# A memory-augmented attention and a squared-ReLU layer on one core: the first segment's tail turns, value tails, softmax of the tokens and last output-weight loads are put in another order

## The chip, the cores and the metric

The kernel runs on one core of a Trainium2 chip. The metric is the device time of one execution in microseconds (us). Engines are named as in the profile: PE is TensorE's matrix multiplication, PEld its weight load, DVE is VectorE, ACT is ScalarE, POOL is GpSimd, SP is the engine whose queue issues most of the DMAs.

## The reference

`x` has 2048 rows of 640, bf16. The first layer is attention in 64 segments of 32 rows, in order, each with 8 memory rows in front; the memory of a segment is the output of the one before. The second layer is a squared ReLU.

```python
def _A_ref(x, mem0, Wq, Wk, Wv, Wo, seg_len):      # H = 32 heads of Dh = 128
    ...
    mask = (idx[:, None] < M) | (idx[:, None] >= idx[None, :])
    mem = mem0
    for s in range(n_seg):
        xs = x[:, s * seg_len:(s + 1) * seg_len, :]
        h = jnp.concatenate([mem, xs], axis=1)       # 8 + 32 rows
        q, k, v = h @ Wq, h @ Wk, h @ Wv             # per head
        scores = jnp.where(mask, q @ k.T * Dh ** -0.5, -1e9)
        o = softmax(scores) @ v
        o = jnp.einsum('bhte,hed->btd', o, Wo)
        mem = o[:, :M, :]
        outs.append(o[:, M:, :])
    return jnp.concatenate(outs, axis=1)
...
h = x + _A_ref(layernorm(x), mem0, Wq, Wk, Wv, Wo, 32)
return h + (relu(layernorm(h) @ w1 + b1) ** 2 @ w2 + b2)
```

## The kernel before

All four attention weights (5.24 MB each) stay on the chip. Four segments make a block of 128 rows; `step(b, sp)` emits segment `s = 4 b + sp`. The order of instructions is written out by hand: each engine runs its own list strictly in the order in which the code emits it, and engines wait for each other by semaphores.

**Main rows and tail rows.** A segment depends on the one before only through 8 memory rows. So in `step` the projections take the 8 memory rows and the first 24 rows of the segment (32 rows in all, "main"), and the last 8 rows of every segment ("tail") are projected separately, 16 segments' tails per layer norm: groups `("t", 0)` to `("t", 3)`, four blocks each. `hTt` holds the turned tail group. Tail projections of q, k and v for a block come from `tail_units` (ten units: two halves `n` of five row chunks `c`, 4 matmuls each with 512 columns) or from `tail_quarters` (20 matmuls of 256 columns in three units). PE runs them as filler: `run(fill, n)` takes the next `n` units from the list `fill` at fixed places in `step`.

**What a unit's end does.** `evac_row` (L264, L266) copies the PSUM tile to a row buffer on ACT; for q and k, `flip` (L269) turns it on DVE, for own rows at once, for tail rows when the list `late` is run; for v the row is stored to `vt_d` in memory, from there `tails_v_in` (L416) reads it back in another layout. Row buffers are four (`rowtile`). Value rows of the start are kept in tiles that are free for the moment (`parked`) and stored later (`stores`, let go by `soon` at the start of a segment, SP, L363).

**Segment 0 and the start.** `start` streams Wv, Wq and Wk against the first segment's main and tail rows as the slices of the weights land (`stream`, tile `pa`), with tail units in between (`units`). Then `step(0, 0, v0)` runs with `ready` true: scores of the 8 memory rows in two halves (`scores`, `sm`; maximum `mx`, exponential `em`, L503 and L506), `token_scores` (tile `sk`), values (`po`), the output projection in rounds (`wo_rounds`, tile `pw`, needs `wo`), and the token softmax (`tk` in three DVE steps at L612 to L615, exponential `ek` on ACT, L633, sum `zk`, L635). `mem_to_hT` turns the memory rows of `pw` (`otr`, L297; `otc`, L298; `hT`, L300), and the next segment's q projection waits for that. In `before`, fill is taken in segment 0 after the first token scores (5 units), after the second (5), before the output rounds (1), after rounds 6 and 7 (5), after 8 to 11 (10), and the rest at the end. `ln_norm(("t", 2))` (tile `xn`, L191) is emitted at the end of `start`, and its transposition `pt` on PE with two copies to `hTt` on ACT (L221) is the eleventh element of `fill`.

**Which value tails are dealt where.** Blocks 1 to 6 in `start`. The list `halves` (L839) deals 6, 2, 2 and 1 halves to segments 0, 1, 2 and 3; `quarters` (L841) gives one quarter to segment 3 and one to each third segment of later blocks.

**Weight loads.** `load_wo` issues Wo in six DMAs on SP: two of 8 heads, four of 4 heads. Rounds 0 to 7 need the first two, rounds 8 to 11 the next two, rounds 12 to 15 the last two.

**Halved matmuls.** `matmul` counts PE's instructions in `issued`; `align` sets `halved[0]`, the number of projection matmuls of 512 columns that `proj` issues as two of 256, so that a given place of each segment falls on a given place in blocks of 256 instructions.

```python
    def align(s, ahead):
        short = -(issued[0] + s + ahead + AHEAD + PLACE) % BLOCK
        halved[0] = short // 2 if short <= 128 else 0
```

After the 64 segments, the second layer runs in four tiles of 512 rows.

## Time and profile before

| | us |
|---|---|
| three runs | 952.0, 954.98, 955.44 (median 954.98) |
| the profiled execution, its own time | 954.06 |
| its span, first to last instruction | 952.2 |
| PE busy | 923.5 (97%) |
| DVE, ACT, POOL busy | 702.1 (74%), 547.5 (57%), 256.4 (27%) |
| PE's share of the chain that ended last | 92% |
| granted TensorE clock | 0.999 |

The span is from the first to the last instruction; the time holds 1.9 us around it. A row of the timeline gives the start, the length, the engine, the line of the code, the operation, the output and inputs by the program's names, and how many instructions are merged; in brackets stands how long the engine had been idle and what ended that. L116 is the line of the helper that issues every matmul, so PE's rows are told apart by their tiles. A row of the stretches gives the length, and for each engine its busy time and number of instructions, then the granted clock, the DMA engines' busy share and GB/s. The chain in order of time follows the work that ended last back from its end; "issue" is time in which an engine waited for nothing that the profile shows.

### The profile page before, as it was taken

What the parts mean: (1) busy time and instruction counts of PE and PEld (TensorE: products, weight loads), DVE (VectorE), ACT (ScalarE), POOL (GpSimd) and SP (SyncE); (2) the same over time, 40 slices, a digit from 0 to 9 for tenths busy, and PEclk for the clock granted to TensorE, in tenths of its full rate; (3) what the DMA queues carried; (4) which work ended last, traced back from release to release, by engine and by line L of the source; (5) the groups of instructions that cost most, each with busy time, mean ns of one, the idle gap of its engine ahead of it and who ended that gap; (6) DMA issues with size and microseconds to landing.
All of it is one profiled execution on the core that took longest, in us unless ns stands there. A gap on an engine that the chain in (4) does not pass through costs nothing.

```text
span 952.2 us, 57555 instructions
## 1 busy us (share of the span) xinstructions
PE 923.5 (97%) x25883; PEld 571.5 (60%) x25883; DVE 702.1 (74%) x2136; ACT 547.5 (57%) x1343; POOL 256.4 (27%) x798
## 2 busy tenths in 40 slices
PE   4989999999999999999999999999999998999998
PEld 2546666666676657666666666666666556555555
DVE  3167888888878888888888888878888888566632
ACT  2456666666666666666666666656666665523321
POOL 1013222222222222222222222222222233253200
PEclk9999999999999999999999999999999999999999
DMA  9973210101010101010101010101010111643220
GB/s 359 397 239 90 46 29 17 27 15 28 14 28 11 34 9 35 9 34 9 33 10 34 9 34 9 31 12 32 12 32 11 53 43 21 211 102 90 90 56 29
DMA packets 60838, 56.74 MB, mean 60 GB/s; under 512 B 27696, under 2 KB 56752, under 8 KB 58672
## 3 DMA queue, kind: packets, MB, share of 16 engines
q1 hardware_dynamic: 59712, 52.73, 18.4%
q8 instruction: 202, 3.31, 1.4%
q10 hardware_dynamic: 880, 0.34, 0.1%
q14 instruction: 44, 0.36, 0.1%
HBM read 38.37 MB, written 9.44 MB: 50 GB/s over the span
## 4 chain that ended last, share of the span: by engine, by line
PE 92%; DMA 5%; DVE 2%; ACT 1%; issue 1%; ACTq 0%; SPq 0%; DVEq 0%
PE ps L116 63%; PE pw L116 16%; PE y L116 6%; PE po L116 5%; DMA wk<-in_A_Wk_dram 2%; PE sm L116 1%; DMA wq<-in_A_Wq_dram 1%; DMA ht<-in_A_x_dram 1%; DMA om<-in_A_mem_dram 1%; DVE wk L938 0%; ACT otc L298 0%; DVE lnst L173 0%; DVE otr L297 0%; DVE kTt L269 0%; DVE hT L300 0%
## 5 line engine op out<-in xcount | busy, mean ns | idle before, releaser
L116 PEld LDWEIGHTS <-hT 128*32 128x32 bf16 x8383 | 221.3, 96 | 134.6 <-DVE hT L300 11.2
L116 PE MATMUL pw<-wo,oT 128*32 128x320 bf16 x4224 | 178.8, 301 | 0.2
L116 PE MATMUL ps<-wv,hT 128*32 128x512 bf16 x2520 | 177.6, 380 | 0.0
L116 PE MATMUL ps<-wq,hT 128*32 128x512 bf16 (+1 forms) x3168 | 160.7, 336 | 5.3 <-DVE hT L300 5.3
L116 PE MATMUL ps<-wk,hT 128*32 128x512 bf16 (+1 forms) x2575 | 160.0, 374 | 0.0
L641 POOL TENSOR_TENSOR pkt<-ek,rk 128x64 bf16<-128x64 bf16 x64 | 19.2, 300 | 416.6 <-DVE rk L639 403.4
L116 PEld LDWEIGHTS <-oT 128*32 128x32 bf16 x4224 | 97.1, 96 | 54.1 <-DVE oT L255 19.6
L269 DVE STREAM_TRANSPOSE qT<-row 128x512 bf16<-128x512 bf16 x128 | 89.8, 702 | 24.0 <-ACT row L264 20.8
L264 ACT ACTIVATE row<-ps 128x512 bf16<-128x512 f32 (+1 forms) x170 | 94.0, 562 | 15.3 <-PE ps L116 12.1
L937 ACT ACTIVATE wv<-ps,b1f 128x512 bf16<-128x512 f32 (+1 forms) x56 | 37.5, 672 | 67.0 <-PE ps L116 66.4
L442 ACT CAST oT<-po 128x512 bf16<-128x512 f32 x128 | 74.7, 586 | 0.0
L298 ACT COPY otc<-otr 64x40 f32<-64x40 f32 x126 | 28.0, 223 | 65.7 <-DVE otr L297 65.2
L453 POOL COPY qz<-qT 128x96 bf16<-128x96 bf16 x126 | 33.3, 264 | 114.6 <-DVE mx L503 57.8
L116 PEld LDWEIGHTS <-hTt 128*32 128x32 bf16 x1640 | 45.0, 97 | 29.0 <-issue 1.5
L635 DVE TENSOR_REDUCE zk<-ek 128x8 f32<-128x320 bf16 x64 | 31.1, 486 | 42.5 <-ACT ek L633 42.5
L266 ACT CAST row<-ps 128x512 bf16<-128x512 f32 (+1 forms) x113 | 61.6, 559 | 1.3 <-PE ps L116 0.5
L116 PEld LDWEIGHTS <-v 32*128 32x128 bf16 x4064 | 42.0, 91 | 33.1 <-issue 18.9
L116 PE MATMUL y<-wq,wk 128*128 128x320 bf16 x448 | 61.4, 299 | 0.4 <-DVE wk L938 0.4
L484 ACT CAST row<-ps 128x256 bf16<-128x256 f32 x126 | 40.7, 375 | 30.9 <-PE ps L116 30.9
L606 ACT CAST v<-ps 128x512 bf16<-128x512 f32 x63 | 36.9, 585 | 29.9 <-PE ps L116 29.9
L116 PEld LDWEIGHTS <-qz 128*32 128x32 bf16 x2016 | 36.6, 95 | 27.5 <-ACT em L506 1.9
L116 PEld LDWEIGHTS <-wk 128*128 128x128 bf16 x448 | 40.5, 98 | 20.8 <-issue 5.0
(109 smaller groups left out, 1626.3 us busy)
## 6 DMA issues: line engine op xcount, KB each, us to landing
wv<-in_A_Wv_dram SPq DMA_DIRECT2D x5, 1024.0 KB
wq<-in_A_Wq_dram SPq DMA_DIRECT2D x5, 1024.0 KB
wk<-in_A_Wk_dram SPq DMA_DIRECT2D x5, 1024.0 KB
vt<-vt_d SPq DMA_DIRECT2D x60, 64.0 KB
xt<-in_A_x_dram SPq DMA_DIRECT2D x18, 160.0 KB
wo<-in_A_Wo_dram SPq DMA_DIRECT2D x2, 1280.0 KB
wo<-in_A_Wo_dram SPq DMA_DIRECT2D x4, 640.0 KB
wq<-in_B_w_dram SPq DMA_DIRECT2D x1, 2080.0 KB
```

Source lines behind the costliest of these rows:

```text
L116: nc.tensor.matmul(*a, **k)
L264: nc.scalar.mul(out=row, in_=ps, mul=scale)
L266: nc.scalar.copy(out=row, in_=ps)
L269: nc.vector.transpose(out=dst[:, n * 16:(n + 1) * 16, 0:32], in_=row.rearrange("p (h e) -> p h e", e=32))
L298: nc.scalar.copy(out=tc_[:, a], in_=tr[64:128, a, :, 0:M])
L442: nc.scalar.copy(out=oTg[:, n, :, :, M:NK], in_=po[:, :, n * 128:(n + 1) * 128].rearrange("p g (j q) -> p g j q", q=32))
L453: nc.gpsimd.tensor_copy(out=d.rearrange("p a (j f) -> p a j f", j=3)[:, :, :, 0:M], in_=src[:, :, 0:3, :])
L484: nc.scalar.copy(out=row[:, u * 256:(u + 1) * 256], in_=ps[:, u * 256:(u + 1) * 256])
L606: nc.scalar.copy(out=v[:, 512:1024], in_=ps1[:])
L635: nc.vector.tensor_reduce(out=zk[:], in_=ek[:], op=ALU.add, axis=AX.X)
L641: nc.gpsimd.tensor_tensor(out=pkt[:], in0=ek[:, :, SEG:NK], in1=rk[:].unsqueeze(2).to_broadcast([128, HG, TL]), op=ALU.mult)
L937: nc.scalar.activation(out=r[:, 0:w], in_=ps[:, 0:w], func=ACT.Relu, bias=b1f[:, fc:fc + 1], scale=1.0)
```

## The change

All of it is in the start and in the first block; the functions of the later segments keep what they emit.

- Wo's last two loads of four heads become four of two heads, in the order in which rounds 12 to 15 use them.
- While Wk streams, `late` is run after the units of each slice, so the tail turns of q of block 1 are emitted there. Behind the last slice only the turn of the row just evacuated is run (`late.pop()()`), so the four turns of k's own rows and tails come first. The two tail turns of k of block 1 stay in `late` and are run in segment 0 behind the second `soft2`, ahead of `tk`.
- `halved[0] = 109` ahead of q's stream: 109 matmuls of the q and k streams and of q's tails are issued as two halves.
- `ln_norm(("t", 2))` and the row loads of group 3 move from the end of `start` to behind the first token scores.
- Fill in segment 0: 4 units after the first token scores, 5 after the second, 1 before the output rounds, 10 after rounds 6 and 7 (the first of them the transposition of tail group 2), all but 6 of the rest after rounds 8 to 11, 6 at the end.
- In segment 0 the token exponential and its sum (`tokens_sum`) are emitted behind rounds 6 and 7 instead of behind round 15.
- Value tails: 7, 1, 1 and 1 halves to segments 0 to 3, and a quarter each to segments 1, 2 and 3. For the seventh half the normalization's tile `xn` serves as one more row buffer, and eight stores instead of seven are let go at the start of segment 1.

```diff
-        for h0, k in ((0, 8), (16, 8), (1, 4), (17, 4), (9, 4), (25, 4)):
+        for h0, k in ((0, 8), (16, 8), (1, 4), (17, 4), (9, 2), (25, 2), (13, 2), (29, 2)):
...
-        row = parked.pop(0) if kept else rowtile()[:]
+        row = parked.pop(0)() if kept else rowtile()[:]
...
-        run(late, 10 if b in (0, NB - 2, NB - 1) else 2)
+        if not ready:
+            run(late, 10 if b in (0, NB - 2, NB - 1) else 2)
...
-        run(late, 1)
+        if not ready:
+            run(late, 1)
...
-        run(late, 10)
+        if not ready:
+            run(late, 10)
...
         token_scores(0)
         if ready:
-            run(fill, DC)
+            ln_norm(("t", 2))
+            load_tail_rows(3)
+            run(fill, 4)
...
             pT1 = soft2(1)
+        if ready:
+            run(late, 100)
         tk = s1.tile([128, HG, NK], F32, tag="tk", name="tk")
...
+        ek = s1.tile([128, HG, NK], BF16, tag="ek", name="ek")
+        zk = s1.tile([128, HG], F32, tag="zk", name="zk")
+
+        def tokens_sum():
+            nc.scalar.activation(out=ek[:], in_=tk[:], func=ACT.Exp, scale=1.0)
+            nc.vector.tensor_reduce(out=zk[:], in_=ek[:], op=ALU.add, axis=AX.X)
...
         wo_rounds(main, pw, 6, 8)
-        run(fill, DC if ready else 1)
+        if ready:
+            tokens_sum()
+        run(fill, 2 * DC if ready else 1)
         wo_rounds(main, pw, 8, 12)
         if ready:
-            run(fill, 2 * DC)
+            run(fill, len(fill) - 6)
         wo_rounds(main, pw, 12, 16)
 
-        ek = s1.tile([128, HG, NK], BF16, tag="ek", name="ek")
-        nc.scalar.activation(out=ek[:], in_=tk[:], func=ACT.Exp, scale=1.0)
-        zk = s1.tile([128, HG], F32, tag="zk", name="zk")
-        nc.vector.tensor_reduce(out=zk[:], in_=ek[:], op=ALU.add, axis=AX.X)
+        if not ready:
+            tokens_sum()
...
+        parked.append(lambda: s1.tile([128, D], BF16, tag="xn", name="vrow")[:, 0:512])
...
                     run(units, k)
+                    run(late, 100)
...
                     tail_out(0, which, n, pa[:, 2 + n, :])
-                    run(late, 100)
+                    late.pop()()
                     tails_in(0, 0, which, n * 16, (n + 1) * 16)
...
+        halved[0] = 109
         stream("q", wq, qT, 7)
...
         run(units, 2 * DC)
-        run(late, 100)
-        ln_norm(("t", 2))
-        load_tail_rows(3)
         return v
...
-    halves = [h for b in range(7, 12) for h in (tail_units(b, "v")[:DC], tail_units(b, "v")[DC:])]
-    halves.append(tail_units(12, "v")[:DC])
-    quarters = [(b, "v", n, u) for b in range(12, NB) for n in range(2) for u in range(2)][2:]
+    halves = []
+    for b in (7, 8, 9, 10, 11, 12):
+        parts = tail_units(b, "v")
+        halves += [parts[:DC], parts[DC:]]
+    del halves[-1], halves[8]
+    quarters = [(11, "v", 0, 0), (11, "v", 0, 1)] + [(12, "v", 1, u) for u in range(2)]
+    quarters += [(b, "v", n, u) for b in range(13, NB) for n in range(2) for u in range(2)]
...
-                for h in range((6, 2, 2, 1)[sp]):
+                for h in range((7, 1, 1, 1)[sp]):
                     fill += halves.pop(0)
                 if sp == 0:
                     fill.insert(2 * DC, lambda: ln_transpose(("t", 2))())
+                else:
+                    fill += tail_quarters(*quarters.pop(0))
                 if sp < 3:
-                    soon.append(lambda n=(7, 5, 5)[sp]: [stores.pop()() for _ in range(min(len(stores), n))])
+                    soon.append(lambda n=(8, 5, 5)[sp]: [stores.pop()() for _ in range(min(len(stores), n))])
...
                 if sp == 3:
                     ln_turn(1)
-                    fill += tail_quarters(*quarters.pop(0))
```

More of the change, by code (lines that the diff above doesn't have):

```diff
@@ L712, with park @@
     f1T = ck(FC * NT).rearrange("p (c t) -> p c t", c=FC)
-    parked = [hnT0[:, c, :] for c in range(DC)] + [ht0[k][:, 0:512] for k in range(3)]
-    parked += [oTts[k][:, 16 * u:16 * u + 16, :].rearrange("p h e -> p (h e)") for k in (1, 0) for u in range(2)]
+    parked = []
+    def park(ap):
+        parked.append(lambda: ap)
+    for c in range(DC):
+        park(hnT0[:, c, :])
+    for k in range(3):
+        park(ht0[k][:, 0:512])
+    for k in (1, 0):
+        for u in range(2):
+            park(oTts[k][:, 16 * u:16 * u + 16, :].rearrange("p h e -> p (h e)"))
     for b in range(2):
         vt4s[b] = s2.tile([128, 4, 2, E], BF16, tag="vt4", name="vt4")
-    parked += [vt4s[1][:, 2 * u:2 * u + 2].rearrange("p s u e -> p (s u e)") for u in range(2)]
+    for u in range(2):
+        park(vt4s[1][:, 2 * u:2 * u + 2].rearrange("p s u e -> p (s u e)"))
     hnTs = [hnT0[:], ck(DC * NT).rearrange("p (c t) -> p c t", c=DC)]
@@ L770, in start @@
         hT4s[1] = s2.tile([128, DC, 4, SEG], BF16, tag="hT4", name="hT4")
-        parked.append(hT4s[1][:, 0:4].rearrange("p c s t -> p (c s t)"))
-        parked.extend(vs[0][:, 512 * u:512 * u + 512] for u in range(2))
+        park(hT4s[1][:, 0:4].rearrange("p c s t -> p (c s t)"))
+        for u in range(2):
+            park(vs[0][:, 512 * u:512 * u + 512])
+        parked.append(lambda: s1.tile([128, D], BF16, tag="xn", name="vrow")[:, 0:512])
         main = lambda c: hT4s[0][:, c, 0, :]
```

## The prediction

> **What bounds the kernel now.** I read the page first: TensorE (PE) is busy 97% of the span and is 92% of the chain that ended last, so only places where PE idles, or where PE work disappears, can move the time. Next came the busy time by stretch, cut where segments begin (segment 0's end from the last Wk slice, then segments 1, 2, 3):

> ```profile
> core 0: us, PE busy (x) PEld busy (x) DVE busy (x) ACT busy (x) POOL busy (x), PEclk, DMA share, GB/s
> 45.50:63.73 18.23, 13.99 (x350) 7.62 (x350) 11.00 (x32) 9.67 (x21) 1.38 (x4) 1.00 0.88 294
> 63.73:76.03 12.30, 12.30 (x371) 7.00 (x374) 10.07 (x33) 6.91 (x18) 3.62 (x13) 1.00 0.32 88
> 76.03:88.32 12.29, 12.29 (x389) 7.38 (x384) 10.03 (x33) 7.99 (x21) 3.97 (x14) 1.00 0.40 105
> 88.32:100.98 12.66, 12.12 (x387) 7.14 (x379) 8.65 (x29) 7.65 (x20) 3.17 (x11) 1.00 0.39 106
> ```

> Segment 0 holds 18.23 - 13.99 = 4.24 us of PE idle; segments 1 and 2 hold none, segment 3 holds 0.54. The timeline of segment 0 names the idle stretches in brackets:

> ```profile
> 50.15 0.28 PE L116 MATMUL sm<-kT,qz 128*32 128x40 bf16 x16 [1.40 <-POOL kT L404]
> 53.03 0.28 PE L116 MATMUL sm<-kT,qz 128*32 128x40 bf16 x16 [1.39 <-ACT em L506]
> 55.17 1.59 ACT L221 COPY hTt<-pt 128x256 bf16<-128x256 bf16 x2
> 56.75 0.23 PE L116 MATMUL po<-pTm,v 32*128 32x8 bf16 x10 [0.45 <-issue]
> 63.73 1.26 PE L116 MATMUL ps<-wq,hT 128*32 128x512 bf16 x21 [0.93 <-DVE hT L300]
> ```

> The chain in order of time says why: the first two are VectorE (DVE) turning tails before the softmax, the last is the token softmax standing ahead of the memory's turn:

> ```profile
> 47.97 1.19 DVE qTt L269 x2
> ...
> 50.86 1.26 DVE kTt L269 x2
> 52.12 0.33 DVE xn L191
> 52.45 0.12 DVE mx L503
> ...
> 61.81 0.38 ACT ek L633
> ...
> 62.62 0.35 DVE otr L297
> ```

> Last, PE's rows at two segment ends: 32 wide value matmuls fill segment 1's end, 16 wide and 20 of half width segment 3's:

> ```profile
> 74.30 1.90 PE L116 MATMUL ps<-wv,hTt 128*32 128x512 bf16 x32
> ...
> 98.85 1.58 PE L116 MATMUL ps<-wv,ht 128*32 128x512 bf16 x36
> 100.98 1.27 PE L116 MATMUL ps<-wq,hT 128*32 128x512 bf16 x35 [0.55 <-DVE hT L300]
> ```

> **Until the last Wk slice (45.54): nothing.** 109 wide matmuls are issued as two halves each. Twenty wide ones take 1.08 us (77.11 to 78.19), so 0.054 each; 32 halves take 0.87 (76.24 to 77.11), so 0.027 each: same work. What small excess there is lies under PE's 0.83 us wait for that slice; without that cover even 2 ns more per half would be 0.2 us. The two q tail turns (1.19 us at 47.97) go into DVE's 8.7 us idle time before 46.14. From segment 3 on PE's instruction list is the same as before, 256 places later, so the steady part is costed at nothing; if the place in the list did matter, a gap like the 0.45 us at 56.30 could recur in each of 60 segments, which is in the chance of anything else.

> **Segment 0, scores.** ScalarE (ACT) evacuates k's rows from 46.64. The four row buffers are no longer held by q's tails, so its 0.29 us wait at 48.00 goes. DVE: k turn 47.25 to 47.96, then three turns at 0.6 each: tail 48.56, second k turn 49.2, its tail 49.8. POOL copies the first k tail at 48.62 (0.06 behind the turn, 0.29 long, as at 49.81), so the first scores start at 48.96 instead of 50.15. The maximum follows at 49.8 instead of 52.36; the exponential must wait for ACT's six evacuations of 0.585 (46.64 to 50.1), so 50.12 instead of 52.59. The second scores come 0.44 later, as at 53.03: 50.56. The tail normalization (xn, 0.4) runs behind the maximum, under the exponential. Its four row loads stay behind Wo's loads on SP's queue and were not waited for; at segment 1's start they are, and had landed by 63.75, so they still fit.

> **Values.** Fill of 20 from 50.8, values at 52.0 (1.20 later, as 53.25 to 54.45), oT cast 0.38 on (52.36), second pTm ready 1.06 after that (53.4). Output rounds 0 to 5 need the second Wo load, which landed at 53.15 by the trace: 53.2 to 54.1 instead of 55.17 to 56.17. So about 2 us have been gained here.

> **Where the gain goes.** Two changes now meet. The last two k tail turns (1.26) run behind pTm and ahead of tk: tk's three DVE steps start at 54.5 and take 1.5 (55.81 to 57.31 before), so they end at 56.05. And the token exponential ek is now issued in ACT's list ahead of the two copies of the turned tail group (hTt, L221); before, it came after all evacuations. ACT therefore stands at ek until 56.07, runs it in 0.47, and makes the copies at 56.5 (0.74) and 57.0 (1.11). Queued behind them are every value tail evacuation and, on PE, all further fill. PE turns the group at 55 and then idles until 57.3, runs 8 matmuls, and idles again until 58.1. From there it has 92 wide matmuls (4.99 us) and 32 output matmuls (1.10, as 73.20 to 74.30) before segment 1: 64.2. The other path, last output round to PE, is pw's end at 63.1 plus 1.17 (74.47 to 75.64 in segment 1): 64.27. Zk no longer stands before otr, so the 0.9 of idle at the end goes, but the start is 64.27 instead of 63.73: **+0.54**, with one more half of value tails (20 x 0.054 = 1.08) inside. If ACT did not hold the copies, PE would run on from 55.9: 100 x 0.054 + 1.10 gives 62.4, **-1.3**; the upper end is a second stall of the size seen at 56.30, **+1.1**. I take +0.54, each step having its own row.

> **Wo in two-head loads.** Landings by the trace: 49.55, 53.15 (1280 KB each), 54.95, 56.83, 58.64, 60.33 (640 KB each): 3.60 us for twice the bytes of 1.8, so splitting costs nothing visible, and PE asks for the last four loads only at 62.5. Both ends: the first half lands 0.85 earlier (no use, so 0), or each 320 KB load takes as long as a 640 KB one (last at 63.9, +1.2). I take 0. [...]

> **Segments 1 to 3.** Segments 1 and 2 each get a quarter (20 half-width matmuls) for a half: -20 x 0.027 = -0.54, less 0.05 because the four matmuls that covered oT before the output rounds (71.01) are gone (segment 3, without them, waited 0.06). After pw the fill lasts 0.87 + 0.54 = 1.41, the memory's turn needs 1.34, so PE still sets the pace: **-0.49** in segment 1. Segment 3 ends on the transposed x of the next block (0.55 idle at 100.44), issued on SP behind the value stores which start from segment 2's end; segment 2's gain can be lost in that wait (0) or kept (-0.49). One of those stores is now half as large, so I take **-0.3**. The quarters after that are 13 as before.

> **Sum.** 0.54 - 0.49 - 0.30 = -0.25 us. On the profiled execution (span 952.2, time 954.06) that is 953.8. The three runs are 952.0, 954.98, 955.44; the middle of all four times is 954.52, so I forecast 954.3.

> **Rivals.**
> A, faster: the hTt copies are not held, as tk is ready by 55 (1.1 us before my count) or ek does not block. For: 4.24 us of idle were there to take. Against: ACT's list has ek first and DVE has 1.26 us of turns ahead of tk. 954.52 - 1.3 - 0.49 - 0.3 = 952.4.
> B, slower: PE's gap without a releaser (0.45 at 56.30; instruction supply is my reading) comes back in the second scores, the same number of instructions into the stream. It then delays exponential, pTm, tk, ek and the copies together. It decides if PE stops more than 0.1 us at about 50.6. For: DMA is full there as it was at 56. [...] +0.6: 954.9. [...]
> C, slower: the small Wo loads cost as much as the larger; it decides from a last landing after 62.8. +1.2: 955.5.

> **How the numbers follow.** Forecast 0.52, A 0.20, B 0.20, C 0.04, anything else 0.04. All cases lie within 0.5% (4.8 us, about what a measurement of this kernel can tell from no change). Range: A less 1.4 and C plus 1.5 for the runs' own scatter (952.0 to 955.44): 951 to 957. Only the unnamed 0.04 and the scatter's tails leave 0.5%: faster 0.02, slower 0.03.

> **What would show it.** In the changed profile: first scores near 49.0; no kTt turn before mx; ek at 56 with the hTt copies directly behind it; PE idle about 1.9 us before the first wide matmul on the new hTt and 0.4 before its ninth; no wait for Wo after 54; segment 1 starting at 64.3, segments 1 and 2 lasting 11.8 each, segment 3 12.7 to 12.9. I am wrong if segment 1 starts before 63.3 (A) or after 65, if PE waits for Wo in rounds 12 to 15 (C), or if the time from segment 4 to the end differs by over 1 us.

## The result and the profile after

The changed kernel takes 957.76 us (median of 12 executions, 955.48 to 960.5) against 954.65 (12 executions, 952.0 to 955.85) of the kernel before: ratio 1.0034, 95% interval 1.0023 to 1.0046. It is slower by 3.1 us, where 0.25 us less had been forecast. The profiled execution took 956.79, with a span of 955.0 (952.2 before) and a mean granted clock of 0.996 (0.999).

The busy time by stretch, cut where segments 1, 2, 3 and 4 begin (first column the stretch, then its length, then busy time of each engine, granted clock, DMA share, GB/s):

```profile
core 0: us, PE busy (x) PEld busy (x) DVE busy (x) ACT busy (x) POOL busy (x), PEclk, DMA share, GB/s
45.50:67.51 22.01, 18.32 (x370) 8.52 (x370) 10.02 (x30) 9.66 (x22) 1.39 (x4) 0.84 0.73 248
67.51:79.40 11.89, 11.89 (x372) 7.17 (x372) 9.80 (x32) 6.99 (x19) 3.59 (x12) 1.00 0.37 102
79.40:91.47 12.07, 12.00 (x392) 9.28 (x388) 9.91 (x33) 7.82 (x21) 3.97 (x13) 1.00 0.39 102
91.47:104.37 12.90, 12.12 (x392) 7.25 (x384) 8.94 (x30) 7.78 (x20) 3.24 (x11) 1.00 0.36 96
```

Segment 1 starts 3.78 us later (67.51 against 63.73). Segment 1 is 0.41 shorter, segment 2 0.22 shorter, segment 3 0.24 longer, and the time from segment 4 to the end 0.59 shorter (850.63 against 851.22): 3.78 - 0.41 - 0.22 + 0.24 - 0.59 = 2.80, the difference of the spans. All of the loss but segment 3's 0.24 us lies in segment 0, and the first row says where to look: PE is busy for 18.32 us instead of 13.99, of which the 20 matmuls more explain some 1.1 us, and the clock is 0.84 instead of 1.00. PE's timeline of that stretch (start, length, engine, line, operation, tiles, number; in brackets the idle time before and what ended it):

```profile
49.15 0.28 PE L116 MATMUL sm<-kT,qz 128*32 128x40 bf16 x16 [0.22 <-POOL kT L404]
...
50.49 0.46 PE L116 MATMUL sm<-kT,qz 128*32 128x40 bf16 x16
50.77 0.28 PE L116 MATMUL ps<-kT,qT 128*32 128x40 bf16 x16
50.87 1.27 PE L116 MATMUL ps<-wv,hTt 128*32 128x512 bf16 x20
52.07 0.26 PE L116 MATMUL po<-pTm,v 32*128 32x8 bf16 x16
52.19 0.18 PE L116 MATMUL po<-pTm,vt 32*128 32x32 bf16 x4
52.30 0.40 PE L116 MATMUL ps<-wv,hTt 128*32 128x512 bf16 x4
52.79 0.31 PE L116 MATMUL pw<-wo,oT 128*32 128x320 bf16 x2
53.36 0.99 PE L116 MATMUL pw<-wo,oT 128*32 128x320 bf16 x22 [0.26 <-DMA wo<-in_A_Wo_dram]
54.29 0.26 PE L116 MATMUL po<-pTm,v 32*128 32x8 bf16 x16
54.40 0.18 PE L116 MATMUL po<-pTm,vt 32*128 32x32 bf16 x4
54.51 0.46 PE L116 MATMUL pw<-wo,oT 128*32 128x320 bf16 x8
54.90 0.28 PE L120 MATMUL pt<-ident,xn 128*128 128x128 bf16 x2
57.25 0.50 PE L120 MATMUL pt<-ident,xn 128*128 128x128 bf16 x3 [2.06 <-issue]
58.55 4.05 PE L116 MATMUL ps<-wv,hTt 128*32 128x512 bf16 x36 [0.81 <-ACT hTt L221]
62.39 1.24 PE L116 MATMUL pw<-wo,oT 128*32 128x320 bf16 x16
```

Down to 54.9 the rows come within 0.25 us of the forecast, but for two output matmuls that run 0.41 us early, ahead of the wait for Wo. Then PE stops in the middle of the transposition `pt`, with two of its five matmuls done, for 2.06 us and without a releaser. ACT's timeline shows that the token exponential was over by then, so that the `hTt` copies waited for `pt`:

```profile
56.15 0.47 ACT L628 ACTIVATE ek<-tk 128x320 bf16<-128x320 f32 x1 [1.23 <-DVE tk L622]
57.79 1.59 ACT L221 COPY hTt<-pt 128x256 bf16<-128x256 bf16 x2 [1.17 <-PE pt L120]
```

From the copies to segment 1 the same work takes 67.51 - 58.55 = 8.96 us. In a run below in which the clock held (e3_both) it takes 63.85 - 56.88 = 6.97. The stretches of 1 us show why (the number behind the brackets is the granted clock):

```profile
56.00:57.00 1.00, 0.00 (x0) 0.00 (x0) 0.46 (x2) 0.47 (x1) 0.00 (x0) 0.82 1.07 369
57.00:58.00 1.00, 0.50 (x3) 0.24 (x3) 0.14 (x1) 0.21 (x1) 0.00 (x0) 0.50 1.07 367
...
62.00:63.00 1.00, 1.00 (x20) 0.51 (x16) 0.00 (x0) 0.00 (x0) 0.00 (x0) 0.50 0.25 79
63.00:64.00 1.00, 1.00 (x24) 0.55 (x20) 0.00 (x0) 0.10 (x1) 0.00 (x0) 0.77 0.14 47
```

The rows left out between them have 0.50 too. Stretches cut finer have 1.00 up to 56.63, 0.50 from there to 63.46 and 1.00 again behind it: 6.83 us at half speed.

So there are two losses on top of the forecast's 0.54: the fill starts at 58.55 instead of 57.3 (1.25), and it runs at half clock (8.96 - 6.97 = 1.99). 0.54 + 1.25 + 1.99 = 3.78. The experiments ask what stopped PE, what held the copies, and what the clock cost.

### The profile page after: what moved, and what is told of

Its sections match the earlier page's. It is cut to its first block, busy times and chain, and to the rows that moved or that the text cites. A ratio compares the mean times of both kernels' runs of the same rounds, so it can differ in the third digit from the quotient of the medians.

```text
span 955.0 us, 57816 instructions
## 1 busy us (share of the span) xinstructions
PE 927.4 (97%) x26011; PEld 568.4 (60%) x26011; DVE 700.4 (73%) x2136; ACT 548.6 (57%) x1344; POOL 257.2 (27%) x798
## 4 chain that ended last, share of the span: by engine, by line
PE 92%; DMA 4%; DVE 1%; ACT 1%; issue 1%; ACTq 0%; DVEq 0%
PE ps L116 62%; PE pw L116 16%; PE y L116 6%; PE po L116 5%; DMA vt_d<-row 2%; PE sm L116 1%; DMA wo<-in_A_Wo_dram 1%; DMA om<-in_A_mem_dram 1%; DMA vt<-vt_d 1%; PE pa L116 1%; ACT otc L298 0%; ACTq L157 0%; DVE otr L297 0%; DVE wk L969 0%; ACT row L266 0%
## 5 line engine op out<-in xcount | busy, mean ns | idle before, releaser
L116 PEld LDWEIGHTS <-hT 128*32 128x32 bf16 x8422 | 217.1, 96 | 137.9 <-DVE hT L300 10.4
L116 PE MATMUL pw<-wo,oT 128*32 128x320 bf16 x4224 | 179.7, 301 | 0.5 <-DMA wo<-in_A_Wo_dram 0.3
L116 PE MATMUL ps<-wv,hT 128*32 128x512 bf16 x2520 | 177.4, 380 | 0.0
L116 PE MATMUL ps<-wq,hT 128*32 128x512 bf16 (+1 forms) x3167 | 160.4, 336 | 4.5 <-DVE hT L300 4.5
L116 PE MATMUL ps<-wk,hT 128*32 128x512 bf16 (+1 forms) x2575 | 159.8, 374 | 0.0
L116 PEld LDWEIGHTS <-oT 128*32 128x32 bf16 x4224 | 97.3, 96 | 55.4 <-DVE oT L255 19.7
L269 DVE STREAM_TRANSPOSE qT<-row 128x512 bf16<-128x512 bf16 x128 | 89.8, 702 | 23.1 <-ACT row L264 20.9
L298 ACT COPY otc<-otr 64x40 f32<-64x40 f32 x126 | 28.2, 224 | 65.2 <-DVE otr L297 64.8
L116 PEld LDWEIGHTS <-hTt 128*32 128x32 bf16 x1729 | 47.2, 98 | 29.1 <-issue 2.7
L116 PE MATMUL y<-wq,wk 128*128 128x320 bf16 x448 | 61.2, 299 | 0.2 <-DVE wk L969 0.2
L116 PEld LDWEIGHTS <-v 32*128 32x128 bf16 x4064 | 42.0, 91 | 32.4 <-issue 18.2
L116 PEld LDWEIGHTS <-wk 128*128 128x128 bf16 x448 | 40.5, 98 | 20.4 <-issue 5.0
L116 PEld LDWEIGHTS <-qz 128*32 128x32 bf16 x2016 | 35.7, 95 | 26.1 <-issue 0.5
```

The source lines that it names most:

```text
L116: nc.tensor.matmul(*a, **k)
L269: nc.vector.transpose(out=dst[:, n * 16:(n + 1) * 16, 0:32], in_=row.rearrange("p (h e) -> p h e", e=32))
L298: nc.scalar.copy(out=tc_[:, a], in_=tr[64:128, a, :, 0:M])
```

## The experiments

Three theories, which fit together, and their rivals. T1: the stop is a fetch of PE's instructions. T2: the token exponential holds the copies as well, so each block hides the other. T3: the clock falls because PE idles. Each ratio below is against the kernel before on the same chip; the rows come from different chips, so their ratios are to be compared and not their medians. Each kernel was profiled once; "stop" is PE's longest idle time without a releaser and "wait" the longest with one, both between 51 us and segment 1's projections.

| run | stop | wait | clock at 0.50 | segment 1 starts | median | ratio (95%) |
|---|---|---|---|---|---|---|
| before | 0.45 | 1.39 | no | 63.73 | 954.65 | |
| after | 2.06 | 0.81 | yes | 67.51 | 957.76 | 1.0034 (1.0023 to 1.0046) |
| e1_place | 0.99 | 2.49 | yes | 67.47 | 958.32 | 1.0023 (1.0007 to 1.0040) |
| e2_ek | 2.63 | 0.81 | yes | 67.08 | 957.42 | 1.0028 (1.0009 to 1.0046) |
| e3_both | 0.78 | 0.81 | no | 63.85 | 956.31 | 1.0002 (0.9987 to 1.0017) |
| e4_wo_half | none | 2.49 | yes | 69.98 | 965.37 | 1.0089 (1.0062 to 1.0115) |
| e5_warm | 0.93 | none | no | 65.79 | 957.75 | 1.0026 (1.0009 to 1.0043) |
| e6_wo_old | 2.53 | 0.81 | yes | 68.48 | 957.81 | 1.0032 (1.0020 to 1.0044) |
| e7_turn_early | 0.98 | none | no | 63.49 | 955.17 | 1.0001 (0.9990 to 1.0012) |
| e8_before_place | 1.47 | 1.38 | no | 65.17 | 956.30 | 1.0018 (1.0006 to 1.0029) |
| e9_wo_held | 0.51 | 2.44 | yes | 66.72 | 956.34 | 1.0033 (1.0018 to 1.0048) |
| e10_held_early | none | 1.92 | yes | 67.35 | 957.79 | 1.0048 (1.0031 to 1.0066) |
| e11_held_less | none | 2.09 | yes | 67.11 | 956.82 | 1.0017 (0.9999 to 1.0034) |
| e12_early_place | 1.57 | none | no | 63.11 | 956.00 | 1.0017 (1.0002 to 1.0032) |

**One block at a time, then both.** e1_place moves every place of PE's list after q's stream by 32 matmuls or 64 instructions:

```diff
-        halved[0] = 109
+        halved[0] = 77
```

> 77 instead of 109 split matmuls in the start (the missing 32 are split in segment 1, so the stream after it is the same): everything in segment 0 stands 64 instructions nearer to the start of PE's list, nothing else changes. Theory T1 (PE's list comes in blocks of 256 instructions, and a block asked for while the DMA engines are full takes some 6.5 us from the crossing before it, so PE stops for 2.06 us in the middle of the transposition at 55.2): the stop leaves the transposition, which runs unbroken near 54.9 to 55.2; the copies of the turned group then wait for ek only and start at 56.6 instead of 57.8; segment 1 starts near 66.3 if the clock falls to half for 6.8 us all the same (PE is still idle from 55.2 to 57.3), near 64.3 if it does not; time 1.2 to 3.2 us below the changed kernel's 957.8. Theory T2 (ek's place in ScalarE's list is what costs): the idle of PE before the first fill on the new group stays at 2 us or more, and segment 1 starts at 66 to 67.5.

e2_ek lets the transposition and its copies go ahead of the token exponential, e3_both does both:

```diff
         if ready:
+            run(fill, 1)
             tokens_sum()
-        run(fill, 2 * DC if ready else 1)
+        run(fill, 2 * DC - 1 if ready else 1)
```

> The token exponential ek is issued behind the two copies of the turned group instead of ahead of them; PE's list is that of the changed kernel. T1: the stop of about 2 us in the transposition stays, the copies start at 57.8 as before, since ek was over at 56.6 anyway; segment 1 starts at 67.5 plus or minus 0.3 and the time is the changed kernel's, 957.8 plus or minus 1. T2: the copies start at 55.3, PE idles under 1 us, segment 1 starts at 63.0, and the time is 953.3.

> Both edits: 77 split matmuls, and ek behind the copies. T1 and T2 together: no stop in the transposition, copies at 55.3, first fill on the new group at 56.1, PE idle there 0.9 us, clock stays at 1.00, segment 1 starts near 63.0, so 4.5 us earlier than in the changed kernel; time 953.2, about 1.4 us below the kernel before. If T1 alone holds (ek is worth nothing), the run is like the one with 77 alone.

PE's timeline of e1_place, of e2_ek and of e3_both:

```profile
52.61 1.26 PE L116 MATMUL ps<-wv,hTt 128*32 128x512 bf16 x18 [0.99 <-issue]
...
59.00 0.62 PE L116 MATMUL ps<-wv,hTt 128*32 128x512 bf16 x8 [2.49 <-ACT hTt L221]
```

```profile
57.67 0.34 PE L120 MATMUL pt<-ident,xn 128*128 128x128 bf16 x3 [2.63 <-issue]
```

```profile
52.17 1.26 PE L116 MATMUL ps<-wv,hTt 128*32 128x512 bf16 x18 [0.78 <-issue]
...
56.88 0.61 PE L116 MATMUL ps<-wv,hTt 128*32 128x512 bf16 x8 [0.81 <-ACT hTt L221]
...
63.85 0.40 PE L116 MATMUL ps<-wq,hT 128*32 128x512 bf16 x4
```

In e1_place the stop has left `pt` and stands, shorter, inside the second fill; but the exponential now holds the copies for 2.49 us, and segment 1 starts where it did. In e2_ek the order is mended and the stop stays in `pt`. With both done, the start moves by 3.66 us and the clock stays at 1.00. Either remedy alone moves it by 0.04 or 0.43 us: T2 holds. By ratio e3_both is the same as the kernel before, so the 1.4 us below it that were expected are not there: the fill on the new group starts at 56.88 instead of 56.1, behind the stop of 0.78, and segment 1 at 63.85 instead of 63.0.

**Less Wo traffic.** e4_wo_half leaves out the odd heads of Wo (a GpSimd fill with zeros instead of their loads):

```diff
+        nc.gpsimd.memset(wo[:, 1:H:2, :], 0.0)
-        for h0, k in ((0, 8), (16, 8), (1, 4), (17, 4), (9, 2), (25, 2), (13, 2), (29, 2)):
+        for h0, k in ((0, 8), (16, 8)):
```

> The odd heads of Wo (half of its bytes, the last 2.6 MB of the start's loads) are filled with zeros by GpSimd at 8 to 18 us instead of loaded; this part of the result is left out. PE's list is that of the changed kernel, the block crossings included. T1: the DMA engines are free from about 53, so the block asked for at 50.6 comes in time or at most 0.5 us late: the stop in the transposition falls from 2.06 to under 0.5 us; the copies start at 56.6; segment 1 starts at 64.3 (clock 1.00) to 66.3 (clock at half for 6.8 us). Rival to T1 (the stop is not the supply of instructions but belongs to the transposition or its buffer): the stop stays at 2 us.

No stop in `pt` (five matmuls in a row at 58.91), as T1 has it, with the DMA engines at a share of 0.20 from 58 to 60. But everything came some 4 to 4.6 us later (output rounds 6 and 7 at 58.52 instead of 54.51), which I put down to the fill on GpSimd, and its executions spread from 958.68 to 965.59. It is no clean test; e9_wo_held is the better one.

**The clock alone.** e5_warm is e1_place with 32 matmuls behind `pt` whose result nobody reads, so that PE doesn't idle while it waits for the copies:

```diff
-                    fill.insert(2 * DC, lambda: ln_transpose(("t", 2))())
+                    def turn_and_warm():
+                        ln_transpose(("t", 2))()
+                        ps = mmtile()
+                        for i in range(8):
+                            for k in range(4):
+                                matmul(ps[32 * k:32 * k + 32, :], lhsT=..., rhs=wv[:, 512 * k:512 * k + 512], ...)
+                    fill.insert(2 * DC, turn_and_warm)
```

> The kernel after with 77 instead of 109 matmuls split in q's stream (as in the run with the moved block crossing alone) and 32 extra wide matmuls into a PSUM tile that nobody reads, right behind the transposition of tail group 2; the token exponential stays ahead of the hTt copies. So PE has the same wait for the copies (58.3 to 58.7), but spends most of it on work that is thrown away (32 x 0.054 = 1.7 us). This isolates the granted clock's share. Theory (the clock fell to 0.50 because PE idled over 2 us, and the 36 wide matmuls behind it cost 2 us more for that): idle in front of the first new fill under 1 us, clock 1.00 throughout segment 0, segment 1 starts at 65.2 to 65.7 instead of 67.47, time 956.0 to 957. Rival (the clock fall has another cause, or cost nothing because PE waits for something else then): clock falls again or segment 1 starts at 67.2 to 67.8, time 958.

A row of its stretches, in the place where e1_place had 0.89 and then 0.50:

```profile
58.00:60.00 2.00, 1.16 (x20) 0.44 (x23) 0.49 (x1) 1.62 (x3) 0.00 (x0) 1.00 0.83 289
```

The 0.84 us of idle time in it is another stop without a releaser. The copies come when they did (58.06, against 58.25), the clock holds, and segment 1 starts at 65.79 instead of 67.47: the half clock cost 1.7 us. T3 holds for the start of segment 1. The ratios (1.0026 and 1.0023) don't show the gain: their intervals overlap.

**Wo's old loads.** e6_wo_old:

```diff
-        for h0, k in ((0, 8), (16, 8), (1, 4), (17, 4), (9, 2), (25, 2), (13, 2), (29, 2)):
+        for h0, k in ((0, 8), (16, 8), (1, 4), (17, 4), (9, 4), (25, 4)):
```

> The kernel after with the kernel before's Wo loads: two of four heads at the end instead of four of two heads. PE's list is that of the kernel after to the instruction. Theory (the two-head loads cost and bring nothing): the 2.06 us stop inside the transposition stays, the clock falls to 0.50, segment 1 starts at 67.5 give or take 0.3, time 957.8 give or take 1. Rival (the split loads feed the late part of segment 0, by fewer fixed costs or by holding back the block of instructions): segment 1 starts 0.6 us or more from 67.5, or the stop changes by over 0.3 us.

The same ratio as the changed kernel (1.0032 against 1.0034), and the same two blocks. In the one profiled execution the stop is 0.47 longer and segment 1 starts 0.97 later, which are the signs that the rival named; but in e2_ek, with the new loads, the stop was also longer (2.63), so one profile of each doesn't tell the loads from chance. In time the split of the loads shows no cost, as forecast, and no gain.

**The place of the crossing in the kernel before.** e8_before_place puts `halved[0] = 77` ahead of q's stream in the kernel before and changes nothing else.

> The kernel before with 77 matmuls split in q's stream and nothing else changed: the same work, 77 instructions more ahead of segment 0, and the list of later segments 256 places on, as in the kernel after. Theory (the gaps without a releaser are crossings of blocks of 256 instructions and move with the place in the list): the 0.45 us gap at 56.30 in the values is gone, a stop of 0 to 1 us appears some 154 matmuls from there, segment 1 starts 63.3 to 64.0, the time from segment 4 on is unchanged, time within 0.1% of the kernel before. Rival (the later place of the steady part's list costs time itself, and that is what makes the kernel after slower): segment 1 starts near 63.7, but the time from segment 4 to the end is 2 us or more longer, ratio 1.002 or more.

PE's timeline:

```profile
60.02 0.45 PE L116 MATMUL pw<-wo,oT 128*32 128x320 bf16 x7 [1.47 <-issue]
...
65.17 1.05 PE L116 MATMUL ps<-wq,hT 128*32 128x512 bf16 x28 [0.92 <-DVE hT L300]
```

The 0.45 us gap in the values is gone, and a stop of 1.47 us stands in the output rounds, larger than the theory's 0 to 1. It stands 10 + 4 + 8 + 20 + 9 = 51 matmuls behind the old place, not the 154 of the expectation: 77 matmuls more bring a crossing 77 matmuls earlier in the work, and the next one, with 128 to a block, comes 128 - 77 = 51 later. Moving places in the list, with the same work, costs the kernel before 0.18%. By the rival the part from segment 4 on should be longer: it is 3.3 us longer (854.55 against 851.22) in this one execution, the slowest of its ten, so that rival isn't excluded here; the changed kernel, at the same places, has 850.63.

**Earlier turn.** e7_turn_early is the changed kernel with 77 splits and the transposition ahead of output rounds 0 to 5:

```diff
-            run(fill, 1)
+            run(fill, 2 if ready else 1)
...
-        run(fill, 2 * DC if ready else 1)
+        run(fill, 2 * DC - 1 if ready else 1)
```

> The kernel after with 77 splits, and the transposition of tail group 2 with its two hTt copies taken ahead of output rounds 0 to 5, so that the copies stand ahead of the token exponential in ScalarE's list and the fill's first value matmuls need not wait for it. Theory (both blocks lifted: the block crossing is out of the transposition, the copies do not wait for the exponential): copies done by 55.5, PE gaps before the fill under 1 us each, clock 1.00, segment 1 starts at 62 to 63 (63.73 in the kernel before, 67.51 after), segment 1 lasts 11.8 to 12.1, time 1 to 2 us below the kernel before: ratio 0.998 to 0.9995. Rival (what was gained goes into the next wait: the memory's turn or Wo's last loads): segment 1 starts at 63.5 to 64.3 all the same, ratio 1.000 give or take 0.0015.

The copies start at 54.24 and the clock is 1.00, but a second stop (0.98 at 57.38) stands in the fill: segment 1 starts at 63.49, and the ratio is 1.0001. Both numbers are the rival's, but by another cause: what took the gain is the stop, not the memory's turn or Wo's last loads.

**The transfers that delay the fetch.** e9_wo_held lets Wo's last six loads go only when the first `oT` cast is done. PE's list is that of the changed kernel.

```diff
+            if ready:
+                for h in (1, 17, 9, 25, 13, 29):
+                    nc.gpsimd.tensor_copy(out=wo[:, h, 0:1], in_=oT[:, 0, 0:1])
+                load_wo(((1, 4), (17, 4), (9, 2), (25, 2), (13, 2), (29, 2)))
+                load_tail_rows(3)
```

> The kernel after, with Wo's last six loads (heads for rounds 8 to 15) issued only when the first oT cast is done (about 52.4 instead of 45.5 to 52), so that the DMA engines are free for a moment between about 53.2 and 54.4; six one-column copies on GpSimd tie them to that cast. PE's list is that of the kernel after. Theory (the stop inside the transposition is a block of 256 instructions whose fetch, asked for at 50.6, is slow because Wo's loads fill the DMA engines): the block is there by 54.5, the stop of 2.06 us falls under 0.5; the hTt copies come at 56.6 behind the token exponential, PE idles under 1.7 us, the clock stays at 1.00, segment 1 starts at 64.0 to 64.8 (which is what the prediction said of the kernel after), time 954.5 to 955.5. Rival (the stop has nothing to do with the DMA load): the stop stays over 1.5 us, segment 1 starts at 67 or later, time 957.5 to 958.5.

The DMA queues between 54.6 and 56.0 in the changed kernel, and between 52.6 and 54.1 here (packets, MB, their time as a share of 16 engines' time):

```profile
q1 hardware_dynamic: 406, 0.50, 100.8%
q8 instruction: 1, 0.02, 5.3%
```

```profile
q1 hardware_dynamic: 179, 0.22, 40.5%
q8 instruction: 1, 0.02, 5.3%
```

Queue q8 carries instructions, one packet of 16 KB: 54.72 to 55.90 in the changed kernel, 52.72 to 53.99 here. And PE here:

```profile
51.60 0.27 PE L116 MATMUL sm<-kT,qz 128*32 128x40 bf16 x14 [0.51 <-issue]
...
55.25 0.51 PE L120 MATMUL pt<-ident,xn 128*128 128x128 bf16 x5
58.20 3.88 PE L116 MATMUL ps<-wv,hTt 128*32 128x512 bf16 x36 [2.44 <-ACT hTt L221]
```

`pt` runs through: with the places of the crossings (e8_before_place, and e12_early_place below) T1 is shown. But the rest of the forecast fails: with everything 0.4 to 0.9 us later the exponential ends at 57.54, PE waits 2.44 us for the copies, the ratio (1.0033) is no better than the changed kernel's, and the clock falls:

```profile
58.00:59.00 1.00, 0.80 (x8) 0.12 (x8) 0.06 (x1) 0.99 (x2) 0.00 (x0) 0.70 1.07 396
...
61.00:62.00 1.00, 1.00 (x16) 0.40 (x12) 0.00 (x0) 0.16 (x1) 0.00 (x0) 0.59 1.06 361
```

**Held loads with the earlier turn.** e10_held_early joins e9_wo_held and the reordering of e7_turn_early, with 109 splits; e11_held_less does the same but ties the loads to the first memory exponential (`in_=ems[0][:, 0:1]`), two microseconds earlier.

> The held loads of the run before, and the transposition of tail group 2 ahead of output rounds 0 to 5, so that the hTt copies do not stand behind the token exponential; 109 splits as in the kernel after. Theory (both blocks lifted and the block of instructions in time): no stop over 0.5 us before 58, clock 1.00, segment 1 starts at 61.3 to 62.7 (63.73 in the kernel before), time 953.0 to 954.2, ratio to the kernel before 0.998 to 0.9995. Rival (what is won goes into the next limit: the following block's fetch, asked for at about 54 under full DMA engines, or the later Wo loads): a stop or a wait for Wo of over 1 us between 58 and 62, segment 1 starts at 63 to 64, ratio 1.000 give or take 0.0015.

> As the run with held loads and the early transposition, but Wo's last six loads are let go two microseconds earlier, by the first memory exponential (about 50.4) instead of the first oT cast, so that they follow the second Wo load with hardly a hole. Theory (the earlier hold cost two waits for Wo, 1.92 and 1.49 us, because the loads began too late; what the fetch needs is only that fewer bytes are queued ahead of it at 50.6): the block comes by 53.5, no stop over 0.5 us before 58, waits for Wo under 0.5 us, clock 1.00, segment 1 starts at 61.5 to 62.8, ratio 0.997 to 0.9995. Rival (without a hole in the transfers the fetch is as late as in the kernel after): a stop without a releaser of 1.5 to 2.1 us at about 55, segment 1 starts at 64 or later, ratio 1.000 to 1.003.

PE in e10_held_early:

```profile
59.28 0.31 PE L116 MATMUL pw<-wo,oT 128*32 128x320 bf16 x2 [1.92 <-DMA wo<-in_A_Wo_dram]
61.09 0.72 PE L116 MATMUL pw<-wo,oT 128*32 128x320 bf16 x14 [1.49 <-DMA wo<-in_A_Wo_dram]
```

Neither has a stop, and both wait for Wo instead, e11_held_less for 2.09 and 1.32 us. The rival of e10_held_early was right in the wait for Wo, but segment 1 starts 3.4 us later than it said and the ratio is above its range. In e11_held_less the theory fails, since my reading of the waits, which it was to use, was wrong, and the rival's stop isn't there either. The DMA engines move 279 GB/s there from 52 to 54, 275 from 54 to 56 and 289 from 56 to 57, against 358 to 377 in the changed kernel. Why loads issued from 51.0 on come hardly earlier to PE (59.21) than those issued from 53.4 on (59.28) stays open.

**The same crossing, another instruction.** e12_early_place is the changed kernel with the reordering of e7_turn_early alone.

> The kernel after with one change: the transposition of tail group 2 ahead of output rounds 0 to 5 (the splits stay at 109, Wo's loads as in the kernel after). The block crossing at 55.2 then lies at the end of output rounds 6 and 7 instead of inside the transposition, and the hTt copies are done before it. Theory (the block is ready at about 57.2 whatever stands at the crossing): PE stops at about 55.1 for 1.9 to 2.2 us, now only once (the 0.81 us wait for the copies behind it is gone); segment 1 starts at 64.1 to 64.7 if this one stop leaves the clock at 1.00, at 66 to 67 if the clock falls. Rival (the stop belongs to the transposition itself, its identity matmuls or its tile): the stop is gone with it, segment 1 starts at 62 to 63.

```profile
54.43 0.45 PE L116 MATMUL pw<-wo,oT 128*32 128x320 bf16 x5
56.44 0.32 PE L116 MATMUL pw<-wo,oT 128*32 128x320 bf16 x3 [1.57 <-issue]
...
63.11 1.26 PE L116 MATMUL ps<-wq,hT 128*32 128x512 bf16 x20
```

The stop now stands inside output rounds 6 and 7, so it is not the transposition's own. It is shorter than forecast (1.57), the clock holds, and segment 1 starts 4.4 us earlier than in the changed kernel. The ratio follows only from 1.0034 to 1.0017, some 1.6 us, with overlapping intervals: in this execution segment 4 starts 0.96 before the kernel before's, but the time from there to the end is 2.46 longer (853.68).

No version beats the kernel before; e3_both and e7_turn_early equal it and so regain what the change lost.

## Why the prediction was wrong

- **Until the last Wk slice, scores, values: right.** First scores 49.15 (48.96 forecast), second 50.49 (50.56), values 52.07 (52.0), output rounds 6 and 7 at 54.51.
- **"Where the gain goes": failed, as a sum.** The order of ACT's list was read rightly (`ek` at 56.15, forecast 56.07), and e1_place and e9_wo_held show that wait at 2.49 and 2.44 us once the stop is out of the way. The term was sized +0.54 and measured +3.78. The step that failed is "PE turns the group at 55 and then idles until 57.3", with dense matmuls at full speed behind it. PE stops inside the turn for 2.06 us, so that the fill starts at 58.55, and the clock is then at half until 63.46. Two things were missing, the fetch and the clock.
- **The instruction fetch, rival B, had the right mechanism and the wrong place and price.** It looked at 50.6, and there PE did stop: the second scores took 0.46 instead of 0.28. The price lay one block later. Count from e9_wo_held's row at 51.60, behind the stop, where 14 of the second scores' 16 matmuls are left: 14 + 16 + 20 + 20 + 4 + 24 + 20 + 8 + 2 = 128 matmuls, with their weight loads 256 instructions, to the point in `pt` where the changed kernel stops. In e12_early_place, with five matmuls of `pt` moved ahead, 14 + 16 + 20 + 20 + 4 + 5 + 24 + 20 + 5 = 128 ends at its stop. In e5_warm and e7_turn_early, too, 128 matmuls lie between the two stops.
- **What the removed waits had covered.** PE gets through the 128 matmuls from 50.6 to 55.2 in 4.6 us; the next block is usable 6.6 us after 50.6. In the kernel before, the same count back from the gap at 56.30 ends at about 50.35, and the block is usable 6.4 us later, at 56.75. Of the two waits for the tail turns only the second, 1.39 us, lay between; it gave the fetch time (my reading), and 0.45 was left to see. So the 2 us that the change won in the scores were lost again: PE goes on behind output rounds 6 and 7 at 57.23 in the kernel before and at 57.25 in the changed one. While Wo streamed, instruction supply was the next limit here. I put B's recurrence at 0.6, where its row showed 0.45, and left instruction supply as a reading; the DMA view of the kernel before, cut to the 2 us before the gap, shows the packet (54.17 to 55.30).
- **The clock was not in the sum at all**, though the forecast itself had PE idle for about 1.9 us. e5_warm prices it at 1.7 us, the comparison with e3_both at 2.0.
- **Wo in two-head loads: right at 0** (e6_wo_old, ratio 1.0032 against 1.0034). By the trace's landings in the changed kernel (55.72, 57.45, then 58.29, 59.16, 59.97, 60.80) the four small loads land 0.81 to 0.87 us apart and the larger one just ahead of them 1.73 after its forerunner: two small loads took no longer than one of twice the bytes. Rival C's wait in rounds 12 to 15 doesn't occur.
- **Segments 1 to 3:** -0.41 for segment 1 (forecast -0.49). Segments 2 and 3 gave -0.22 + 0.24 instead of -0.30: segment 3 waits 0.65 instead of 0.55 for the turned memory, the loss that the text named.
- **The steady part** is 0.59 shorter, within the 1 us allowed.

## What to carry to other kernels

Where an engine's waits are removed while the DMA engines are full, count its instructions against the rate at which they were fetched there (in the changed kernel PE ran 128 matmuls in 4.6 us, and the block behind them was usable after 6.6): a removed wait may have been the cover of the next block, and the place of the crossing decided here what it blocked. Two blocks that end close together can hide each other, so removing one tells little about the other's worth (here 0.04 and 0.43 us alone, 3.66 together). A forecast TensorE idle time like those before which the clock fell here (1.6 us or more in one window of 3.41 us, see below), in front of dense matmuls, should carry a price for the clock beside its own length (1.7 to 2.0 us here).

## What the hardware showed that I had not expected

```profile
53.22:56.63 3.41, 1.82 (x52) 1.02 (x51) 2.79 (x7) 0.85 (x3) 0.00 (x0) 1.00 1.07 366
54.42:57.83 3.41, 1.84 (x45) 1.40 (x37) 2.38 (x5) 1.25 (x3) 0.00 (x0) 1.00 1.05 360
```

The ends of matmuls are modelled (by the rows of the timeline the first has 0.26 + 1.45 = 1.7 us), so the border is known to about 0.1 us. In e10_held_early the wait of 1.92 us (57.36 to 59.28) lies in two windows (they meet at 58.63), and the clock falls only at the end of the second, with the next wait in it. In the changed kernel and in e6_wo_old the window behind the fall again has 1.42 and 1.14 us without PE work, and a second one at half speed follows; in the other six it has under 0.3, and the clock comes back after one.
- Open: the time from segment 4 to the end ranges from 849.8 to 855.2 us over these 14 profiled executions. Short stops without a releaser stand there at changing places: 0.21 to 0.57 us at 340.85, 613.68 and 629.91 in the kernel before, 0.23 to 0.51 at 343.53, 439.56 and 728.11 in the changed one. The longest time is that of e2_ek, whose profiled execution was the slowest of its ten, the shortest that of e9_wo_held, the fastest of its ten. The three that start segment 4 earliest (e3_both, e7_turn_early, e12_early_place) have 853.5 to 853.7 there. Whether that is chance, with one profile of each, or has to do with the early start was not tried.
